# Block 0's transposes, logits and dispatch in blocks 1 to 4, two pairs' scores in block 1, weights converted in place

## The chip, the cores and the metric

One Trainium2 chip, one core. The time is the device time of one execution in microseconds, as the median of several runs. The engines of the core: TensorE (PE; PEld is its weight load), VectorE (DVE), ScalarE (ACT), GpSimd (POOL) and SyncE (SP), which here only issues DMA transfers. Each engine works through its own instructions in program order and waits where an operand or a buffer isn't ready.

## The reference

q, k, v are cut into chunks of 64 tokens; each chunk attends to itself only. The attention output (4608 tokens by 512) runs through a layer `w_in` (512 by 2048) with a sigmoid gate and `w_out` (2048 by 512), and then through a "soft" mixture of experts with 32 slots:

```python
h = x @ w_in
g = h * (1.0 / (1.0 + np.exp(-1.702 * h)))
x = g @ w_out
logits = x @ phi
d = softmax of logits over the tokens (axis 0)       # dispatch weights
slot_input = d.T @ x                                  # 32 slots, 4 for each of 8 experts
slot_out = relu(slot_input[e] @ w1[e]) @ w2[e]        # for each expert e
c = softmax of logits over the slots (axis 1)
out = c @ slot_out
```

The weights `w_in` and `w_out` arrive as 64-bit floats and are turned into 32-bit ones on the chip.

## The kernel before

The 4608 tokens are worked in 12 blocks of 384 (`T`). A block has three attention pairs (128 tokens each) and 16 products f = 0 to 15 (`gemm`, L288), one for each 128 columns of `w_in`. A product is 12 matmuls: x and the weights are split into a high and a low part, and three of the four combinations are summed in one of three PSUM tiles "h" (L292 to L294). ACT takes tanh of it (L296), DVE forms g (L297): the evacuation. In blocks 1 to 10 DVE then transposes g in squares of 32 (L307, `store_g`), and after four products SP writes them to DRAM. `w_out` is never multiplied with g directly: `wp` = w_out times phi gives the logits from g (`logits`, L353), and the dispatch sums g itself with the weights d (`dispatch`, L486, after `load_g`, L322, has read the transposed g back).

What is put between the products is written out by hand, in strings: `HEAD` before block 0, `SIDE0`, `SIDE1` and `SIDE2` for blocks 0 to 2 (key: the product behind which the steps stand), and `PLAN` for blocks 2 to 10. The order of every engine and of SP's queue is that order (`manual_schedule`). The steps, in the strings' letters:

- `P a,c` (`pair_step`, L767): the scores of pair a on PE (L216), the values of pair c (L267), both in one PSUM tile "sx" of which there is a single one; then on DVE maximum and difference for a (L227, L228: "the scores" on DVE), on SP the load of the next q and k, and for c ACT's copy xh (L282) and DVE's xl (L283). "-" leaves a side out.
- `e` (`attn_e`, L233): exp on ACT (L235), three small sums on DVE (L237 to L240), the scaling of e on POOL (L241). `b` (`attn_b`, L245): four transposes on PE (L252) into the PSUM tile "m" (a single one) and ACT's copy pt_sb (L254).
- `Li`, `Lo`: loads of tiles of w_in and w_out (`load_w`, L133) into staging tiles. `i`, `I`, `j` (`w_in_a`, `_b`, `_c`): convert a w_in tile (ACT L119, DVE L123 and L126) and split it (ACT L155, POOL L156); block 0 does this for product f + 3 to f + 5. `o` (`wp_a`, L162): the same conversion of a w_out tile (L119, L123, L126).
- `c`, `d` (`wp_c`, `wp_d`): w_out times phi for four converted tiles (L168), in the PSUM tile "m", ACT's copy (L172), then eight matmuls (L179) again in "m" and a copy to `wp` (L182).
- `t` (`store_g` of block 0), `k` (logits of block 0), `l` (logits of block 1), each for four products; `S0` to `S4` (`slots_0` to `slots_b`): the softmax of one block, of which S0 begins with two matmuls in "m" (L378); `g` and `D`: load_g and dispatch of block 0; `s`: a small selection matrix (L762).

The softmax over tokens is carried from block to block: `stat[b]` holds the maximum and the sum so far, and block b rescales with those of block b - 1. In before, block 0 goes first. `w` in `PLAN` (`more_wo`) loads and converts one more tile of w_out in its second layout; in blocks 2 to 9 that happens four times a block (two loads, two conversions). The w_in staging tiles and the split weights share 17 tiles (`wpool`); w_out staging tiles, x, and the transposed g share 11 (`slab`). Converted weights go to six tiles "cv" (`NCV`).

Of the kernel before, what the change touches and what calls it, by code (L numbers as in the profile page):

```python
# [52 lines left out]
def attention_moe_softmoe_kernel(  # L53
# [84 lines left out]
    def conv(kind, f):
        v = pro[0].tile([128, DM], F32, tag="cv", name="cv", bufs=NCV)
        to_f32(v, stg.pop((kind, f)))  # L140
        return v

    iv = {}
# [768 lines left out]
```

## Time and profile before

| | us |
|---|---|
| median of 3 runs (664.71 to 664.84) | 664.83 |
| span of the profiled execution | 664.1 |
| PE busy | 620.1 (93%) |
| DVE busy | 455.0 (69%) |
| ACT busy | 225.3 (34%) |
| POOL busy | 92.2 (14%) |

The times of the runs are those of whole executions; the span is that of one profiled execution from its first to its last instruction. In the profile PE's matmuls overlap (a matmul of 384 columns shows about 0.33 us, and the next one starts 0.17 us later), so what a step costs on PE is read from the starts, not from the durations. A row of the timeline is: start, duration, engine, line, operation, out<-in, shape and count, and in brackets the idle time before it with what ended it.

### The profile page before, as it was taken

The page shows a single profiled execution, that of the slowest core. Times are in us where ns is not written, and L with a number is a line of the kernel's source. Part 1 is how long each engine was busy: PE and PEld are TensorE (multiplying, and loading weights), DVE is VectorE, ACT ScalarE, POOL GpSimd, SP SyncE. Part 2 cuts the span into 40 slices and gives each one's busy share as a digit, 9 for nine tenths or more (in the row PEclk, how much of TensorE's full clock was granted, in tenths as well). Part 3 has the DMA queues.
Part 4 walks back from the last instruction along what each step waited for, and adds up shares of the span by engine and source line. Part 5 has one row for each costly group of instructions (what it writes and reads, how often), then busy time and mean ns, then how long its engine had stood idle before and what let it go on. Part 6 is the DMA issues. An engine that isn't in the chain of part 4 may idle for free.

```text
span 664.1 us, 15558 instructions
## 1 busy us (share of the span) xinstructions
PE 620.1 (93%) x6414; PEld 523.4 (79%) x6414; DVE 455.0 (69%) x975; ACT 225.3 (34%) x471; POOL 92.2 (14%) x117
## 2 busy tenths in 40 slices
PE   4887999999999999999999999999999999979883
PEld 3776865798889897998998979989989798726552
DVE  5798789797858778677787786777876736331033
ACT  3646544333323233333332333333323322121132
POOL 0355200000101000000010000000101112232410
PEclk9999999999999999999999999999999999998997
DMA  9943867669968567496585774965838879789997
GB/s 345 355 144 112 298 210 224 188 167 333 312 200 330 145 228 269 129 316 196 160 332 141 228 272 129 324 188 161 333 87 267 272 250 389 287 291 375 404 416 310
DMA packets 66055, 167.94 MB, mean 253 GB/s; under 512 B 12544, under 2 KB 36224, under 8 KB 65984
## 3 DMA queue, kind: packets, MB, share of 16 engines
q1 hardware_dynamic: 57376, 129.72, 58.6%
q0 software_dynamic: 8608, 37.23, 14.8%
q8 instruction: 50, 0.82, 0.5%
q14 instruction: 21, 0.17, 0.1%
HBM read 122.29 MB, written 44.63 MB: 251 GB/s over the span
## 4 chain that ended last, share of the span: by engine, by line
PE 81%; DVE 9%; ACT 3%; issue 2%; DMA 2%; SPq 0%; POOL 0%; DVEq 0%; ACTq 0%
PE h L292 19%; PE h L294 18%; PE h L293 18%; PE lp L358 5%; PE dtg L492 5%; PE sx L216 3%; PE h1p L653 3%; DVE cv L126 2%; PE sx L267 2%; PE fp L673 2%; PE pt L252 2%; DVE cv L123 2%; DVE gt L297 1%; PE op L706 1%; DMA v<-in_v_dram 1%
## 5 line engine op out<-in xcount | busy, mean ns | idle before, releaser
L292 PE MATMUL h<-xh,w 128*128 128x384 f32 x768 | 266.5, 347 | 2.7 <-ACT w L155 2.2
L294 PE MATMUL h<-xh,w 128*128 128x384 f32 x768 | 258.9, 337 | 5.5 <-POOL w L156 5.5
L293 PE MATMUL h<-xl,w 128*128 128x384 f32 x768 | 258.2, 336 | 0.0
L296 ACT ACTIVATE gt<-h 128x384 f32<-128x384 f32 x192 | 94.0, 490 | 221.5 <-PE h L294 221.3
L292 PEld LDWEIGHTS h<-xh,w 128*128 128x128 f32 x768 | 144.9, 189 | 23.3 <-issue 17.8
L297 DVE SCALAR_TENSOR_TENSOR gt<-gt,h 128x384 f32<-128x384 f32 x192 | 104.9, 547 | 82.1 <-ACT gt L296 81.8
L294 PEld LDWEIGHTS h<-xh,w 128*128 128x128 f32 x768 | 144.8, 189 | 8.0 <-POOL w L156 7.1
L293 PEld LDWEIGHTS h<-xl,w 128*128 128x128 f32 x768 | 145.0, 189 | 0.2 <-DVE xl L283 0.2
L307 DVE STREAM_TRANSPOSE g<-gt 128x384 f32<-128x384 f32 x176 | 100.2, 574 | 5.4
L241 POOL TENSOR_TENSOR e<-e,rs 128x512 f32<-128x512 f32 x33 | 34.5, 1044 | 415.9 <-DVE rs L240 410.5
L282 ACT ACTIVATE xh<-sx 128x512 fp32r<-128x512 f32 (+1 forms) x38 | 21.6, 575 | 96.0 <-DVE e L228 82.4
L283 DVE TENSOR_TENSOR xl<-sx,xh 128x512 fp32r<-128x512 f32 (+1 forms) x38 | 25.0, 661 | 25.3 <-ACT xh L282 23.8
L565 POOL DMA_DIRECT2D w<-in_moe_w_dram x56 | 29.8, 533 | 87.0 <-PE h L294 36.2
L358 PE MATMUL lp<-gt,wp 128*32 128x384 f32 x384 | 36.8, 492 | 0.1
L492 PE MATMUL dtg<-g,dt 128*32 128x512 f32 x288 | 33.2, 594 | 1.4 <-DVE dt L450 1.4
L126 DVE SCALAR_TENSOR_TENSOR cv<-stg,cv 128x512 uint32<-128x512 uint32 x32 | 29.7, 928 | 1.1
L156 POOL TENSOR_TENSOR w<-cv,w 128x512 fp32r<-128x512 f32 x16 | 24.2, 1525 | 37.9 <-ACT w L155 37.9
L227 DVE TENSOR_REDUCE mx<-sx 128x8 f32<-128x512 f32 (+1 forms) x37 | 23.9, 645 | 5.7 <-PE sx L216 5.7
L228 DVE TENSOR_TENSOR e<-sx,mx 128x512 f32<-128x512 f32 (+1 forms) x37 | 25.1, 677 | 1.8
L252 PE MATMUL pt<-ident,e 128*128 128x128 f32 x144 | 23.1, 285 | 3.4 <-DVE e L241 3.2
L715 DVE COPY o<-op 128x512 f32<-128x512 f32 (+1 forms) x20 | 11.1, 630 | 21.1 <-PE op L706 21.1
L492 PEld LDWEIGHTS dtg<-g,dt 128*32 128x32 f32 x288 | 9.0, 110 | 19.6 <-issue 17.9
(117 smaller groups left out, 554.7 us busy)
## 6 DMA issues: line engine op xcount, KB each, us to landing
g_dram<-g SPq DMA_DIRECT2D x176, 192.0 KB, 3.8
g<-g_dram SPq DMA_DIRECT2D x44, 768.0 KB, 8.9
w<-in_moe_w_dram POOLq DMA_DIRECT2D x34, 512.0 KB, 8.7
qk<-in_qk_dram SPq DMA_DIRECT2D x30, 512.0 KB, 5.5
w<-in_moe_w_dram POOLq DMA_DIRECT2D x17, 768.0 KB, 7.8
stg<-in_moe_w_in_dram SPq DMA_DIRECT2D x16, 512.0 KB, 8.4
stg<-in_moe_w_out_t_dram SPq DMA_DIRECT2D x16, 512.0 KB, 6.1
wo<-in_moe_w_out_dram SPq DMA_DIRECT2D x16, 512.0 KB, 3.7
```

Of the source, the lines that this page charges most:

```text
L126: nc.vector.scalar_tensor_tensor(out=a.bitcast(U32), in0=u[:, :, 0], scalar=29, in1=a.bitcast(U32), op0=ALU.logical_shift_right, op1=ALU.b ...
L241: (nc.gpsimd if pool else nc.vector).tensor_tensor(out=e, in0=e, in1=rs.to_broadcast([128, 2 * KD, 64]), op=ALU.mult)
L252: nc.tensor.transpose(p[:, hp, :], e[:, 2 * hp:2 * hp + 2, :].rearrange("p h k -> p (h k)"), ident)
L292: nc.tensor.matmul(out=h, lhsT=a, rhs=xh[b][:, k, :], start=(k == 0), stop=False)
L293: nc.tensor.matmul(out=h, lhsT=a, rhs=xl[b][:, k, :], start=False, stop=False)
L294: nc.tensor.matmul(out=h, lhsT=l, rhs=xh[b][:, k, :], start=False, stop=(k == KD - 1))
L296: nc.scalar.activation(out=t, in_=h, func=ACTF.Tanh, scale=0.851)
L297: nc.vector.scalar_tensor_tensor(out=t, in0=t, scalar=1.0, in1=h, op0=ALU.add, op1=ALU.mult)
L307: nc.vector.transpose(out=g1[b, q][:, :, :, 32 * j:32 * (j + 1)], in_=t.rearrange("p (a b c) -> p b a c", b=4, c=32))
L358: nc.tensor.matmul(out=lp[b][32 * j:32 * (j + 1), :], lhsT=wp[:, f, :], rhs=gt[b, f], start=(g == 0), stop=(g == NG - 1),)
L492: nc.tensor.matmul(out=p[32 * j:32 * (j + 1)], lhsT=dt[:, i, :], rhs=g[j][i], start=(i == 0), stop=(i == NCP - 1))
L565: eng.dma_start(out=t[:, 0:at], in_=w12[:, w_at[0]:w_at[0] + at])
```

## The change

- Pairs 6 and 7: their scores (`P6`, `P7`) move from products 9 and 12 of block 0 to products 0 and 2 of block 1, their softmax (`e6`, `e7`) and `b6` with them; `P8`'s place stays.
- `w_out` conversions `o0` to `o15` are spread, about one behind every product of block 1 (before: two a product, done by product 8). `c0` to `c2` and `d0` to `d2` follow at products 5 to 14, `c3` and `d3` in block 2.
- Block 0's transposes `t` leave block 1: ten stand in block 2, six in block 3. Its logits `k` stand in block 2 at products 8 and 12, its softmax at the end of block 3 and the start of block 4 (S0 behind b3 of block 3), its dispatch at product 4 of block 4.
- The running softmax now begins with block 1, and block 0 comes between blocks 2 and 3 (`FIRST`, `BEFORE`).
- Weights are converted in place: L119 writes back into every second word of the staging tile, L123 works on these, L126 writes the result to the tile's lower half; the "cv" tiles are gone. Six of the w_out loads go into three new tiles ("p"), the others as before into `slab` ("r").
- The tiles of the first stages live to the end of block 3 (`NPRO`), so the second-layout conversions start in block 4, with six instead of four calls a block (`w4`, `w5`).

```diff
-PLAN = (('b1', 2), ('w2', 2), ('w3', 2), ... ('S1', 7), ('p3', 8), ...
-NCV = 6
+PLAN = (('b1', 2), ('w2', 2), ('w3', 2), ... ('S1', 7), ('w4', 7), ('w5', 7), ('p3', 8), ...
+FIRST = 1
+BEFORE = {2: 1, 0: 2, 3: 0}
+NPRO = 4
 SIDE0 = {
...
-    7: "e5 b4 Li13", 8: "Li14 q7", 9: "P6,4 Li15 v7", 10: "e6 b5", 11: "Lo0r", 12: "P7,5 Lo1r", 13: "e7 b6 Lo2r", 14: "Lo3r",
-    15: "Lo4r",
+    7: "e5 b4 Li13", 8: "Li14 q7", 9: "P-,4 Li15 v7", 10: "b5", 11: "Lo0r", 12: "P-,5 Lo1r", 13: "Lo2r", 14: "Lo3r", 15: "Lo4r",
 }
 SIDE1 = {
-    0: "o0 o1 Lo5r Lo6r", 1: "s o2 o3 Lo7r Lo8r", 2: "b7 c0 o4 o5 Lo9r Lo10r", 3: "d0 o6 o7 Lo11r Lo12r", 4: "P8,6 k0 l0 c1 o8 Lo13r",
-    5: "e8 d1 o9 o10 Lo14r Lo15r", 6: "o11 o12", 7: "c2 o13 o14 t0 t1", 8: "P9,7 k1 l1 d2 o15", 9: "e9 c3 t2 t3 t4", 10: "b8 d3 t5 t6 t7",
-    11: "t8 t9", 12: "P10,8 k2 k3 l2 t10", 13: "e10 b9 t11 t12", 14: "S0 t13 t14", 15: "S1 t15",
+    0: "P6,- o0 Lo5p", 1: "e6 o1 s Lo6p", 2: "P7,- o2 Lo7p", 3: "e7 b6 o3", 4: "P8,6", 5: "e8 b7 c0 o4 Lo8r Lo9r", 6: "d0 o5 l0 Lo10r Lo11r",
+    7: "o6", 8: "P9,7 o7", 9: "e9 b8 c1 o8 Lo12r Lo13p", 10: "d1 o9 l1 Lo14p Lo15p", 11: "o10", 12: "P10,8 o11", 13: "e10 b9 c2 o12",
+    14: "d2 o13 l2", 15: "o14 o15",
 }
-SIDE2 = {0: "S2 g", 1: "S3", 3: "S4", 8: "D"}
+SIDE2 = {
+    0: "c3", 1: "d3 t0", 2: "t1", 3: "t2", 5: "t3", 6: "t4", 7: "t5", 8: "k0 k1", 9: "t6", 10: "t7", 12: "k2 k3", 14: "t8", 15: "t9",
+}
+SIDE3 = {1: "t10", 3: "t11", 5: "t12", 7: "t13", 8: "t14", 10: "t15", 13: "S0 G", 14: "S1", 15: "S2"}
+SIDE4 = {0: "S3", 1: "S4", 4: "D"}
...
-    def to_f32_a(a, st):
-        f = st.bitcast(F32).rearrange("p (n w) -> p n w", w=2)
-        nc.scalar.activation(out=a, in_=f[:, :, 1], func=ACTF.Prelu, scale=2.0 ** -112, alpha=-(2.0 ** 32))
+    def to_f32_a(st):
+        f = st.bitcast(F32).rearrange("p (n w) -> p n w", w=2)[:, :, 1]
+        nc.scalar.activation(out=f, in_=f, func=ACTF.Prelu, scale=2.0 ** -112, alpha=-(2.0 ** 32))
     def to_f32_b(a, st):
         u = st.bitcast(U32).rearrange("p (n w) -> p n w", w=2)
-        nc.vector.tensor_scalar(
-            out=a.bitcast(U32), in0=a.bitcast(U32), scalar1=3, scalar2=None, op0=ALU.logical_shift_left
-        )
+        nc.vector.tensor_scalar(out=u[:, :, 1], in0=u[:, :, 1], scalar1=3, scalar2=None, op0=ALU.logical_shift_left)
         nc.vector.scalar_tensor_tensor(
-            out=a.bitcast(U32), in0=u[:, :, 0], scalar=29, in1=a.bitcast(U32),
+            out=a.bitcast(U32), in0=u[:, :, 0], scalar=29, in1=u[:, :, 1],
             op0=ALU.logical_shift_right, op1=ALU.bitwise_or,
         )
+    def low(st):
+        return st.bitcast(F32)[:, 0:DM]
...
     def wp_a(q):
-        ov[q] = conv("o", q)
+        st = stg.pop(("o", q))
+        to_f32(low(st), st)
+        ov[q] = low(st)
...
             elif kind == "w":
-                if 1 < b < 10:
+                if NPRO <= b < 10:
                     more_wo()
...
-            if b < 3:
-                start((SIDE0, SIDE1, SIDE2)[b].get(f, ""))
+            if b < 5:
+                start((SIDE0, SIDE1, SIDE2, SIDE3, SIDE4)[b].get(f, ""))
```

## Rows read from the trace of the kernel before

**Rows 1.** The page: span, and PE's busy tenths in 40 equal slices.
```profile
span 664.1 us, 15558 instructions
...
PE   4887999999999999999999999999999999979883
```

**Rows 2.** PE's timeline: third matmul of product 9 in block 0; block 1; block 2.
```profile
53.57 0.44 PE L294 MATMUL h<-xh,w 128*128 128x384 f32 x1 [1.24 <-POOL w L156]
...
75.69 0.33 PE L292 MATMUL h<-xh,w 128*128 128x384 f32 x1
...
77.77 0.33 PE L292 MATMUL h<-xh,w 128*128 128x384 f32 x1
...
136.14 0.33 PE L292 MATMUL h<-xh,w 128*128 128x384 f32 x1
```

**Rows 3.** PE's timeline in block 1: b7, c0, d0, P8,6, logits, c1.
```profile
81.94 0.60 PE L252 MATMUL pt<-ident,e 128*128 128x128 f32 x4
83.22 1.05 PE L168 MATMUL wpp<-cv,acc 128*32 128x512 f32 x4 [0.69 <-ACT pt_sb L254]
...
88.72 0.97 PE L179 MATMUL wps<-sel,psb 128*128 128x32 f32 x8
89.53 0.42 PE L292 MATMUL h<-xh,w 128*128 128x384 f32 x1
...
91.79 0.69 PE L216 MATMUL sx<-qk 64*64 64x64 f32 x32
92.31 0.65 PE L267 MATMUL sx<-pt_sb,v 64*64 64x64 f32 x32
92.89 1.50 PE L358 MATMUL lp<-gt,wp 128*32 128x384 f32 x16
94.20 1.04 PE L168 MATMUL wpp<-cv,acc 128*32 128x512 f32 x8
```

**Rows 4.** DVE's timeline in block 1.
```profile
78.49 0.56 DVE L297 SCALAR_TENSOR_TENSOR gt<-gt,h 128x384 f32<-128x384 f32 x1 [1.52 <-ACT gt L296]
...
79.59 0.39 DVE L123 TENSOR_SCALAR cv<-cv 128x512 uint32<-128x512 uint32 x1
80.01 0.69 DVE L126 SCALAR_TENSOR_TENSOR cv<-stg,cv 128x512 uint32<-128x512 uint32 x1
80.62 0.42 DVE L123 TENSOR_SCALAR cv<-cv 128x512 uint32<-128x512 uint32 x1
...
94.21 0.65 DVE L227 TENSOR_REDUCE mx<-sx 128x8 f32<-128x512 f32 x1
94.90 0.69 DVE L228 TENSOR_TENSOR e<-sx,mx 128x512 f32<-128x512 f32 x1
96.34 0.69 DVE L283 TENSOR_TENSOR xl<-sx,xh 128x512 fp32r<-128x512 f32 x1 [0.75 <-ACT xh L282]
...
99.52 0.64 DVE L237 TENSOR_REDUCE sm<-e 128x8 f32<-128x512 f32 x1
...
102.29 0.41 DVE L123 TENSOR_SCALAR cv<-cv 128x512 uint32<-128x512 uint32 x1
```

**Rows 5.** POOL's timeline in block 0.
```profile
65.69 3.19 POOL L156 TENSOR_TENSOR w<-cv,w 128x512 fp32r<-128x512 f32 x2
```

**Rows 6.** DVE's timeline in block 0, the same stretch.
```profile
67.75 1.67 DVE L126 SCALAR_TENSOR_TENSOR cv<-stg,cv 128x512 uint32<-128x512 uint32 x1
```

**Rows 7.** PE's timeline in block 3: b3 and what follows.
```profile
223.27 0.60 PE L252 MATMUL pt<-ident,e 128*128 128x128 f32 x4
223.63 0.42 PE L292 MATMUL h<-xh,w 128*128 128x384 f32 x1
```

**Rows 8.** ACT's timeline in block 3, the same stretch.
```profile
223.86 0.63 ACT L235 ACTIVATE e<-e 128x512 f32<-128x512 f32 x1
224.38 0.59 ACT L254 ACTIVATE pt_sb<-pt 128x512 f32<-128x512 f32 x1
```

**Rows 9.** Busy us of each engine in a steady stretch; PE, PEld, DVE, ACT, POOL.
```profile
220.00:264.00 44.00, 44.00 (x454) 39.33 (x450) 33.50 (x74) 15.20 (x32) 3.13 (x3) 1.00 0.67 221
```

More of the change, by code (lines that the diff above doesn't have):

```diff
@@ L113, in to_f32, with load_w @@
     def to_f32(a, st):
-        to_f32_a(a, st)
+        to_f32_a(st)
         to_f32_b(a, st)
-    def to_f32_a(a, st):
-        f = st.bitcast(F32).rearrange("p (n w) -> p n w", w=2)
-        nc.scalar.activation(out=a, in_=f[:, :, 1], func=ACTF.Prelu, scale=2.0 ** -112, alpha=-(2.0 ** 32))
+    def to_f32_a(st):
+        f = st.bitcast(F32).rearrange("p (n w) -> p n w", w=2)[:, :, 1]
+        nc.scalar.activation(out=f, in_=f, func=ACTF.Prelu, scale=2.0 ** -112, alpha=-(2.0 ** 32))
     def to_f32_b(a, st):
         u = st.bitcast(U32).rearrange("p (n w) -> p n w", w=2)
-        nc.vector.tensor_scalar(
-            out=a.bitcast(U32), in0=a.bitcast(U32), scalar1=3, scalar2=None, op0=ALU.logical_shift_left
-        )
+        nc.vector.tensor_scalar(out=u[:, :, 1], in0=u[:, :, 1], scalar1=3, scalar2=None, op0=ALU.logical_shift_left)
         nc.vector.scalar_tensor_tensor(
-            out=a.bitcast(U32), in0=u[:, :, 0], scalar=29, in1=a.bitcast(U32),
+            out=a.bitcast(U32), in0=u[:, :, 0], scalar=29, in1=u[:, :, 1],
             op0=ALU.logical_shift_right, op1=ALU.bitwise_or,
         )
+    def low(st):
+        return st.bitcast(F32)[:, 0:DM]
     pro, stg, w_t = {}, {}, {}
-    def load_w(kind, f, in_slab):
-        t = (slab_tile if in_slab else w_tile)([128, DM], I64, "stg")
+    def load_w(kind, f, place):
+        if place == "r":
+            t = slab_tile([128, DM], I64, "stg")
+        elif place == "p":
+            t = pro[0].tile([128, DM], I64, tag="o", name="stg", bufs=3)
+        else:
+            t = w_tile([128, DM], I64, "stg")
         nc.sync.dma_start(out=t, in_=(w_in if kind == "i" else w_out_t)[:, f, :])
         stg[kind, f] = t
[L138 to L143, printed above, removed]
     def w_in_a(f):
-        iv[f] = pro[0].tile([128, DM], F32, tag="cv", name="cv", bufs=NCV)
-        to_f32_a(iv[f], stg["i", f])
+        to_f32_a(stg["i", f])
     def w_in_b(f):
-        to_f32_b(iv[f], stg.pop(("i", f)))
+        to_f32_b(low(stg["i", f]), stg["i", f])
     def w_in_c(f):
-        v = iv.pop(f).rearrange("p (k c) -> p k c", k=KD)
+        v = low(stg.pop(("i", f))).rearrange("p (k c) -> p k c", k=KD)
         t = w_tile([128, 2, KD, 128], F32R, "w")
@@ L354, in logits @@
         if g == 0:
-            lp[b] = ps.tile([128, T], F32, tag="lp" if b % 2 else "pt", name="lp")
+            lp[b] = ps.tile([128, T], F32, tag="lp" if b % 2 or b == 0 else "pt", name="lp")
         for j in range(4):
@@ L367, in logits @@
                 return
-            lps[b] = [mid_tile([128, T], f"lps{i}", F32R) for i in range(2)]
+            lps[b] = [
+                mid_tile([128, T], f"lps{i}", F32R) if b else pro[0].tile([128, T], F32R, tag="gt", name="lps0", bufs=NF)
+                for i in range(2)
+            ]
             nc.scalar.activation(out=lps[b][0], in_=p, func=ACTF.Copy)
@@ L395, in slots_1 @@
         cr = None
-        if b > 0:
+        if b != FIRST:
             cr = st_p.tile([128, 1], F32, tag="cr", name="cr")
-            nc.scalar.activation(out=cr, in_=stat[b - 1][0], func=ACTF.Exp, scale=-1.0, bias=nm)
+            nc.scalar.activation(out=cr, in_=stat[BEFORE.get(b, b - 1)][0], func=ACTF.Exp, scale=-1.0, bias=nm)
         sm_t[b] = d, nm, s, cr
@@ L494, in dispatch @@
                 )
-        if b == 0:
+        if b == FIRST:
             nc.vector.tensor_copy(acc, p)
@@ L579, in more_wo @@
     def more_wo():
-        fn, i = wo_list.pop(0)
-        fn(i)
+        if wo_list:
+            fn, i = wo_list.pop(0)
+            fn(i)
     def at(key):
@@ L798, in start @@
         once = {
-            "phi": start_wp, "z": start_const, "s": start_sel, "g": lambda: load_g(0), "D": lambda: dispatch(0),
+            "phi": start_wp, "z": start_const, "s": start_sel, "G": lambda: load_g(0), "D": lambda: dispatch(0),
         }
         for x in steps.split():
-            k, n = x[0], x[1:].rstrip("r")
+            k, n = x[0], x[1:].rstrip("rp")
             if x in once:
@@ L805, in start @@
             elif k == "L":
-                load_w(x[1], int(n[1:]), x[-1] == "r")
+                load_w(x[1], int(n[1:]), x[-1])
             elif k in "AC":
@@ L838, in attention_moe_softmoe_kernel @@
             start(HEAD)
-            block(0)
-            block(1)
+            for b in range(NPRO):
+                block(b)
     with tc.tile_pool(name="spare", bufs=NSPARE) as pro[1]:
@@ L843, in attention_moe_softmoe_kernel @@
             more_wo()
-            for b in range(2, NB - 1):
+            for b in range(NPRO, NB - 1):
                 block(b)
```

10 lines of the change are left out of this document (5 added, 5 removed).

## The prediction

> **What bounds the kernel now.** I read the page first, then TensorE's timeline block by block, then the three engines that feed it. The span is 664.1 us [rows 1]; the median of the runs shown is 664.83, so 0.73 us lie around the span, and I carry that over unchanged. In the slices of [rows 1] TensorE is full from the ninth slice to the thirty-fifth; only the head, the early blocks and the tail have gaps. Since the change touches neither head, steady blocks nor tail in their order, what it can win lies in blocks 0 and 1.
>
> A product of a block (12 matmuls of `gemm`) takes 77.77 - 75.69 = 2.08 us [rows 2]. Block 1 runs from 75.69 to 136.14, which is 60.45 us. Its work, from start-to-start distances in [rows 3]: pair (scores and values) 92.89 - 91.79 = 1.10, scores alone 0.52, values alone 0.58; one `b` (four transposes) 223.63 - 223.27 = 0.36 [rows 7]; one `c` 1.04; one `d` 0.81; a logits group (94.20 - 92.89) / 2 = 0.66. Two plain matmuls of S0 are 2 x 2.08 / 12 = 0.35. So 16 x 2.08 + 3 x 1.10 + 3 x 0.36 + 4 x 1.04 + 4 x 0.81 + 7 x 0.66 + 0.35 = 50.0, and **10.4 us are waits** (restarts after an insertion, some 0.1 each, are left in; they stay in the sum after too). They sit at the `c` steps: c0 waits for pt_sb, the copy that empties b7's PSUM tile, and then for DVE's conversions [rows 3].
>
> In block 0 I take the stretch from the third matmul of product 9 (53.57) to block 1, 22.12 us [rows 2]. Ten matmuls of product 9 (1.73), 6 x 2.08, 2 x 1.10 and 2 x 0.36 are 17.1, so **5.0 us are waits**, for weights that are still being split (POOL's L156, as in the 1.24 us that end at 53.57).
>
> TensorE's work as a whole does not change: every matmul that leaves a block comes back in another. So the time changes by waits after minus waits before; 15.4 us of waits before are open to it.
>
> **Prices on DVE** [rows 4]. Evacuation and transposition of one product 79.59 - 78.49 = 1.10, the first starting 78.49 - 77.77 = 0.72 after the product's end (ACT's tanh lies between). Conversion of one w_out tile 80.62 - 79.59 = 1.03. Scores (L227, L228) 1.38. Then ACT copies xh, and L283 ends 96.34 + 0.69 - 95.59 = 1.44 after L228. Softmax sums with a conversion behind them 102.29 - 99.52 = 2.77: while POOL scales e, the two-input L126 is held up. The same holding is seen in block 0: while POOL's two L156 take 3.19 us [rows 5], an L126 takes 1.67 instead of 0.69 [rows 4, 6].
>
> **Part 1: block 0 loses the scores of pairs 6 and 7 and two softmaxes.** That is 2 x (1.38 + 1.01) = 4.8 us of DVE work, and 2 of POOL's multiplications. More than the sum, it is an order that goes: in product 9 ACT copies xh only after DVE's new scores in the same PSUM tile (the 0.75 idle before L283 [rows 4] shows the copy queued between the two), and the splitting of weights is queued behind that copy. With values alone the copy needs no scores. The wait up to 53.57 comes from pair 5, which stays, and is counted on neither side. For products 9 to 11 DVE does an evacuation (half of 1.10), a conversion (1.03) and is held by one L156 (half of 3.19 less the part beside the evacuation, some 1.2): 2.8 a product against 2.1 to 2.7 on TensorE. Over three products that leaves 0.5 to 2; with the last split ending behind the last conversion I take 1.8 instead of 5.0 us: **-3.2**.
>
> **Part 2: block 1.** DVE loses block 0's transposes, all 16, some 8 us (half of 1.10 each), and gains 4.8 us of scores and softmax. The sum falls, but the order decides. I walk from the block's start (TensorE and DVE from 0). First evacuation at 2.8. Product 0: 1.10 + 1.38 + 1.03 = 3.5. Product 1: 1.10 + 2.77 and 0.5 for sel = 4.4. Product 2: 3.5. Product 3: 1.10 + 2.77 = 3.9. DVE is then at 18.1, and reads P8's scores at 18.1 + 1.10 + 1.38 = 20.6. TensorE needs for products 0 to 4 with P6, P7, b6 and P8 only 5 x 2.08 + 2 x 0.52 + 0.36 + 1.10 = 12.9. Behind the scores ACT has, in its order, copy xh, tanh of product 5, exp of e8, and the copy of b7's tile: four steps at the 0.52 distance of [rows 8], so 22.7. c0 may start only then: it uses the single PSUM tile "m" that b7 has filled (the pt_sb wait of [rows 3] is this one, with no exp before it). TensorE's own work up to c0 is 12.9 + 2.08 + 0.36 = 15.3: 7.4 us lost with restarts. c0 ends at 23.7. Products 6, 7, 8 with d0 and l0 follow, 7.9 with restarts, to 31.6. c1 has the same neighbours (P9, e9, b8): 0.72 + 1.10 + 1.38, then five ACT steps (copy xh, o7's first step, tanh, exp, copy) at the same distance make 5.8, so c1 starts at 37.4, where TensorE was free at 35.2. One turn later c2 starts at 38.4 + 7.9 + 5.8 = 52.1, ends at 53.2, and products 14, 15 with d2 and l2 (5.7) close the block at 58.9. Its work is 16 x 2.08 + 2 x 0.52 + 3 x 1.10 + 4 x 0.36 + 3 x 1.04 + 3 x 0.81 + 3 x 0.66 = 46.6. Waits **12.3 instead of 10.4: +1.9**.
>
> **Part 3: blocks 2 to 4.** c3 (block 2, product 0) needs o14 and o15, both put behind product 15: 0.72 + 1.10 + 2 x 1.03 = 3.9 after its end, where TensorE is ready after 2.08: **+1.9**. S0 of block 0 now stands right behind b3 in block 3, again on tile "m": b3's transposes end at 223.63, the copy ends at 224.38 + 0.59 = 224.97 [rows 7, 8], with exp before it: **+1.4**. The ten, then six transposes (0.5 each), the logits groups and the dispatch are work without a wait: block 2 and 3 have no weight conversions of w_out any more (2 x 1.03 fewer each), and DVE is idle for a quarter of a steady block (33.50 of 44 us busy [rows 9]). Three conversions in blocks 4 to 8 instead of two are covered by the same idle time (if it were gone, 1 us a block at most). The loads of block 0's g are queued on SP behind block 3's last stores of block 0, four products ahead of use; if they were late, the dispatch would wait, and only it.
>
> **Part 4: in place.** L123 reads and writes every second word. The trace has no such row. Nearest is L123 itself, 0.39 (same count, packed); the other end is L126, which reads with that step and takes 0.69. Below nothing I see no reason. I take L123's own row, cost 0. A staging tile is held one step longer; w12 to w15 then go into tiles that POOL has read one product before, 2 us ahead: cost 0, up to 1 us if POOL is late. Loads Lo8 and Lo9 wait on SP for c0's tiles, to 23.7; they are needed past 37, which leaves 13 us for a transfer.
>
> [...]
>
> **Sum.** Waits after 1.8 + 12.3 + 1.9 + 1.4 = 17.4, before 15.4: **+2.0 us**, span 666.1, median 666.8 (0.3% slower).
>
> **Rivals.** (a) L123 falls to 0.69: 0.3 x 16 = 4.8 us on a DVE that sets c0 to c3 in block 1; block 0 hardly changes, since L123 there waits for POOL anyway. 4 to 5 us of it show: some 671.5. For it: nothing in the trace excludes it. (b) Faster: DVE keeps pace at P8. The 7.4 us before c0 come from DVE's 17.8 us for products 0 to 4 against TensorE's 12.9. If conversions and softmax sums overlapped so that P8's scores were read at 15 instead of 20.6, c0 would wait 5.5 us less, and the time would be 661.3; it is a gain as soon as more than 2.0 us go there. Against it: the prices are start-to-start distances, with nothing left between; for it: block 1 has 3 us less DVE work in all. (c) No change: parts 1 and 2 cancel; each of the terms may be off by 1 us, which gives 663.5 to 666.1. (d) The change does not do what it says, because w_out tiles land late and conversions wait for DMA: up to 5 us more, 672; the slack of 13 us above speaks against it.
>
> **How the numbers follow.** Forecast (666.2 to 669) 0.41; (a) 0.18; (b) 0.20; (c) 0.18; (d) 0.03. Slower by over 0.2% (1.3 us, about what a measurement of this kernel can tell): 0.41 + 0.18 + 0.03 = 0.62. Within: 0.18. Faster: 0.20. The range goes from (b)'s 661.3 to 672, leaving a tenth at each end; the likeliest case alone is 665.5 to 669.
>
> **What would show it.** Right: block 1 starts near 71, lasts near 59, with c0 starting some 5 us after b7's transposes behind pt_sb; c1 and c2 wait 2 us each; S0's matmul starts 1.4 us after b3's in block 3. Wrong: L123 at 0.69 in the changed kernel (a); c0 right behind b7 and block 1 under 55 us (b); ACT waiting for w_out loads (d). A wait of TensorE beyond block 4 would be a thing I did not see.

## The result and the profile after

The changed kernel takes 675.15 us (median of four runs, 672.85 to 677.89) against 664.79 (664.71 to 664.84) before: a ratio of 1.0149 with a 95% interval of 1.0133 to 1.0166. It is slower, as forecast, but by 10.4 us where 2.0 were forecast.

The lines of the code have moved by a few: L119 is now L124, L123 L128, L126 L129, L168 L173, L179 L184, L252 L257, L254 L259, L292 to L294 L297 to L299, L358 L363, L378 L386.

The page of the changed kernel: span, PE's busy tenths and the clock granted to PE, in 40 slices. It answers to [rows 1].

```profile
span 673.5 us, 15546 instructions
...
PE   3888968899999999999999999999999999988883
...
PEclk9999978899999999999999999999999999999997
```

The head, the steady blocks and the tail look as they did. Slices six to eight (84 to 135 us) have a hole, and in the same slices the granted clock is down to seven and eight tenths; all three lie in block 1. From the starts of PE's first matmul of each block:

| | before | forecast | after |
|---|---|---|---|
| block 1 starts | 75.69 | 71.1 | 71.24 |
| block 1 lasts | 60.45 | 58.9 | 67.45 |
| block 2 lasts | 47.29 | 51.05 | 51.28 |
| block 3 lasts | 44.45 | 46.15 | 46.23 |
| block 4 lasts | 44.32 | 47.0 | 46.88 |
| block 5 starts | 272.20 | 274.2 | 283.08 |

(The forecasts of blocks 2 to 4 are the lengths before with the steps of the prediction's part 3 put in: c3, d3, ten and six transposes, logits, S0 and dispatch.) One block is wrong, by 8.5 us, and all the others are within 0.25.

PE's timeline of the changed kernel in block 1, from its first matmul to that of block 2. It answers to [rows 3].

```profile
71.24 0.33 PE L297 MATMUL h<-xh,w 128*128 128x384 f32 x1
...
88.76 0.66 PE L257 MATMUL pt<-ident,e 128*128 128x128 f32 x4 [0.21 <-POOL e L246]
93.76 2.12 PE L173 MATMUL wpp<-stg,acc 128*32 128x512 f32 x8 [4.35 <-ACT pt_sb L259]
95.82 0.69 PE L297 MATMUL h<-xh,w 128*128 128x384 f32 x1
96.31 0.52 PE L298 MATMUL h<-xl,w 128*128 128x384 f32 x1
96.62 0.52 PE L299 MATMUL h<-xh,w 128*128 128x384 f32 x1
...
99.39 0.33 PE L299 MATMUL h<-xh,w 128*128 128x384 f32 x1
99.56 0.97 PE L184 MATMUL wps<-sel,psb 128*128 128x32 f32 x8
100.90 0.85 PE L363 MATMUL lp<-gt,wp 128*32 128x384 f32 x8 [0.37 <-ACT wp L187]
101.69 0.44 PE L297 MATMUL h<-xh,w 128*128 128x384 f32 x1
...
111.92 1.65 PE L173 MATMUL wpp<-stg,acc 128*32 128x512 f32 x8 [1.98 <-ACT pt_sb L259]
...
129.29 1.95 PE L173 MATMUL wpp<-stg,acc 128*32 128x512 f32 x8 [1.96 <-ACT pt_sb L259]
...
138.69 0.33 PE L297 MATMUL h<-xh,w 128*128 128x384 f32 x1
```

The waits are those of the forecast: c0 starts 93.76 - 71.24 = 22.5 us into the block (forecast 22.7), 5.0 us behind b7's transposes and behind pt_sb; c1 and c2 wait 1.98 and 1.96 us (forecast 2). What is new stands *behind* each wait. Of a product, one matmul starts 96.62 - 96.31 = 0.31 us after the other, where 0.17 is the rule; c0 itself takes 95.82 - 93.76 = 2.06 us instead of the 1.04 of [rows 3]. The distance is back at 0.17 from 99.39 on.

The same kernel in stretches of 10 us: busy time of PE, PEld, DVE, ACT and POOL, then PE's granted clock, DMA's share and GB/s.

```profile
80.00:90.00 10.00, 8.28 (x104) 7.20 (x103) 9.69 (x18) 2.56 (x5) 1.93 (x2) 1.00 0.58 171
90.00:100.00 10.00, 6.24 (x25) 4.58 (x25) 5.39 (x11) 3.38 (x7) 1.04 (x1) 0.66 0.61 194
100.00:110.00 10.00, 9.57 (x117) 8.25 (x116) 6.73 (x13) 3.34 (x8) 0.00 (x0) 1.00 0.62 190
110.00:120.00 10.00, 7.71 (x41) 5.87 (x42) 7.09 (x14) 4.39 (x9) 1.04 (x1) 0.83 0.79 251
120.00:130.00 10.00, 8.04 (x108) 7.22 (x107) 7.09 (x14) 4.08 (x8) 0.00 (x0) 1.00 0.66 189
130.00:140.00 10.00, 9.63 (x54) 7.72 (x49) 5.04 (x12) 3.64 (x8) 1.04 (x1) 0.83 0.03 12
```

The stretches with c0 and c1, and the one behind the start of c2 (129.29), have a mean clock under 1.00; the stretches between are at 1.00. Before, no stretch of block 1 was under 1.00; two of its stretches, of the kernel before:

```profile
80.00:90.00 10.00, 9.10 (x48) 6.17 (x47) 8.47 (x18) 5.13 (x11) 0.00 (x0) 1.00 0.67 222
...
100.00:110.00 10.00, 8.94 (x103) 5.80 (x106) 9.48 (x20) 4.31 (x8) 1.04 (x1) 1.00 0.68 229
```

In shorter stretches the granted clock is 0.50 from 92.5 to 99.0 us and 1.00 again from 99.25 on; behind the start of c1 it is 0.50 from 113.0 to 116.25, behind that of c2 from 130.0 to 133.25, and 1.00 ahead of these stretches and behind them. The rows agree, with 0.31 to 0.33 us between matmuls of 384 columns at 0.50 and 0.17 at 1.00, so 0.66 is a mean over time at these two values.

A second, smaller new row is the logits' wait, 0.37 us for the copy behind `d` (L187). It comes with each of l0 to l2, since `l` stands right behind its `d`.

Why c0 is late, on DVE and ACT of the changed kernel:

```profile
90.94 0.69 DVE L233 TENSOR_TENSOR e<-sx,mx 128x512 f32<-128x512 f32 x1
```

```profile
91.72 0.60 ACT L287 ACTIVATE xh<-sx 128x512 fp32r<-128x512 f32 x1 [5.28 <-DVE e L233]
92.22 0.49 ACT L301 ACTIVATE gt<-h 128x384 f32<-128x384 f32 x1
92.59 0.63 ACT L240 ACTIVATE e<-e 128x512 f32<-128x512 f32 x1
93.11 0.60 ACT L259 ACTIVATE pt_sb<-pt 128x512 f32<-128x512 f32 x1
```

DVE ends P8's scores at 91.63, 20.4 us into the block (forecast 20.6), and ACT does its four steps behind them: copy, tanh, exp, and the copy that gives the PSUM tile "m" back to c0. The walk of the prediction is in these rows step for step. Its price for what TensorE does afterwards is not.

### The profile page after: what moved, and what is told of

Read it like the earlier page. It is cut to its first block, busy times and chain, and to the rows that moved or that the text cites. A ratio compares the mean times of both kernels' runs of the same rounds, so it can differ in the third digit from the quotient of the medians.

```text
span 673.5 us, 15546 instructions
## 1 busy us (share of the span) xinstructions
PE 623.5 (93%) x6414; PEld 526.4 (78%) x6414; DVE 457.8 (68%) x975; ACT 226.1 (34%) x471; POOL 91.3 (14%) x117
## 3 DMA queue, kind: packets, MB, share of 16 engines
q1 hardware_dynamic: 57376, 129.72, 58.1%
## 4 chain that ended last, share of the span: by engine, by line
PE 81%; DVE 10%; ACT 4%; issue 2%; DMA 1%; POOL 0%; SPq 0%; DVEq 0%; ACTq 0%
PE h L297 19%; PE h L299 18%; PE h L298 18%; PE lp L363 5%; PE dtg L500 5%; DVE stg L129 3%; PE sx L221 2%; PE sx L272 2%; PE fp L682 2%; PE h1p L662 2%; PE pt L257 2%; DVE stg L128 2%; DVE gt L302 2%; PE wpp L173 1%; PE op L715 1%
## 5 line engine op out<-in xcount | busy, mean ns | idle before, releaser
L297 PE MATMUL h<-xh,w 128*128 128x384 f32 x768 | 268.2, 349 | 1.5 <-ACT w L158 1.0
L299 PE MATMUL h<-xh,w 128*128 128x384 f32 x768 | 260.1, 339 | 3.9 <-POOL w L159 3.8
L297 PEld LDWEIGHTS h<-xh,w 128*128 128x128 f32 x768 | 146.1, 190 | 24.7 <-issue 20.3
L302 DVE SCALAR_TENSOR_TENSOR gt<-gt,h 128x384 f32<-128x384 f32 x192 | 105.0, 547 | 86.9 <-ACT gt L301 86.4
L299 PEld LDWEIGHTS h<-xh,w 128*128 128x128 f32 x768 | 145.9, 190 | 6.6 <-POOL w L159 5.8
L363 PE MATMUL lp<-gt,wp 128*32 128x384 f32 x384 | 37.0, 492 | 1.2 <-ACT wp L187 1.1
L129 DVE SCALAR_TENSOR_TENSOR stg<-stg 128x512 uint32<-128x512 uint32 x32 | 30.9, 966 | 1.1
L159 POOL TENSOR_TENSOR w<-stg,w 128x512 fp32r<-128x512 f32 x16 | 23.1, 1449 | 36.0 <-ACT w L158 36.0
L257 PE MATMUL pt<-ident,e 128*128 128x128 f32 x144 | 23.2, 286 | 3.9 <-DVE e L246 3.2
```

The lines of the kernel that those rows point to most:

```text
L129: nc.vector.scalar_tensor_tensor(out=a.bitcast(U32), in0=u[:, :, 0], scalar=29, in1=u[:, :, 1], op0=ALU.logical_shift_right, op1=ALU.bitwi ...
L257: nc.tensor.transpose(p[:, hp, :], e[:, 2 * hp:2 * hp + 2, :].rearrange("p h k -> p (h k)"), ident)
L297: nc.tensor.matmul(out=h, lhsT=a, rhs=xh[b][:, k, :], start=(k == 0), stop=False)
L299: nc.tensor.matmul(out=h, lhsT=l, rhs=xh[b][:, k, :], start=False, stop=(k == KD - 1))
L302: nc.vector.scalar_tensor_tensor(out=t, in0=t, scalar=1.0, in1=h, op0=ALU.add, op1=ALU.mult)
L363: nc.tensor.matmul(out=lp[b][32 * j:32 * (j + 1), :], lhsT=wp[:, f, :], rhs=gt[b, f], start=(g == 0), stop=(g == NG - 1),)
```

## The experiments

All times are medians; "before" ran beside each on the same chip, with 664.9 to 665.7 us. A *slot* is the distance from the first matmul of a product to that of the next, with all that stands between. The ladder first, then the clock, then what the waits hang on.

**One part of the change at a time: in place alone.** The kernel before, with the conversion functions of the kernel after and nothing else.

```diff
-        ov[q] = conv("o", q)
+        st = stg.pop(("o", q))
+        to_f32(low(st), st)
+        ov[q] = low(st)
...
-    def to_f32_a(a, st):
+    def to_f32_a(st):
```

> The kernel before with the conversion in place alone, everything else as before (staging tiles are held until the split or the c step). Theory: L123 and L126 keep their durations on every second word (0.39 to 0.43 and 0.69); 664.8, within 0.7. Rival: staging tiles that come free later delay the w_out loads, conversions wait for DMA, 1 to 4 us slower.

Measured: 666.73 us (ten runs), 1.0018 [1.0004, 1.0032] of before: 1.0 us more, at the edge of what can be told. It does not lie in the shift. All instructions of that line on staging tiles in the kernel after, and of its counterpart before; duration min/median/max in ns:

```profile
L128 DVE TENSOR_SCALAR stg<-stg x32: 377/422/1399, 14.4 to 141.5; 128x512 uint32<-128x512 uint32 x32
```

```profile
L123 DVE TENSOR_SCALAR cv<-cv x32: 374/420/1061, 14.4 to 114.8; 128x512 uint32<-128x512 uint32 x32
```

Rival (a) falls: on every second word the operation takes 422 ns in the median, packed it took 420. (On the 16 tiles of the second layout the medians are 388 in place alone and 389 before.)

Where the 1.0 us lies can be read in one execution of each. Block 1 starts 0.80 us earlier in place than before (74.89 against 75.69) and lasts 1.84 us longer (62.29 against 60.45). In it a transposition on DVE stands 1.61 us until PE is done with c1; ACT's copy psb comes later for that, and d1 waits 0.87 us for the copy. Before, neither of the two waits. In place alone (L168 of before is L163 there, L307 is L302):

```profile
94.49 0.58 DVE L302 STREAM_TRANSPOSE g<-gt 128x384 f32<-128x384 f32 x1 [1.61 <-PE wpp L163]
```

```profile
97.61 1.08 PE L174 MATMUL wps<-sel,psb 128*128 128x32 f32 x8 [0.87 <-ACT psb L167]
```

In place, the converted weights lie in the staging tile itself, so a `slab` tile comes free only behind the `c` that reads it, and this transposition is given one of those. Before, the tile was free behind its conversion. So tiles do come free later, as the rival of the expectation had it, but it is DVE that waits and not a load. The next run, which has the same order, shows the same two waits (0.97 and 0.86 us). The clock does not show as the reason: product 9 of block 0 takes 6.31 us in place and 4.91 before, at a granted clock of 0.82 and 1.00 between 50 and 55 us, but block 1 starts no later for it, and over all runs the mean granted clock is 0.990 in both kernels.

**The transposes, logits, softmax and dispatch of block 0 alone** (with in place, and with the tiles of the first stages living to the end of block 3): the order of blocks 0 and 1 as before, without block 0's `t`, `k`, S0 and S1 in block 1.

```diff
+    0: "o0 o1 Lo5r Lo6r", 1: "s o2 o3 Lo7r Lo8r", 2: "b7 c0 o4 o5 Lo9r Lo10r", 3: "d0 o6 o7 Lo11r Lo12r", 4: "P8,6 l0 c1 o8 Lo13r",
+    5: "e8 d1 o9 o10 Lo14r Lo15r", 6: "o11 o12", 7: "c2 o13 o14", 8: "P9,7 l1 d2 o15", 9: "e9 c3", 10: "b8 d3",
+    12: "P10,8 l2", 13: "e10 b9",
```

> The changed kernel with block 0 and block 1 in the order of the kernel before (pairs 6 and 7 in block 0, w_out conversions two a product, c0 to c3 at products 2, 4, 7, 9), so that only block 0's transposes, logits, softmax and dispatch are moved and the conversion is in place. Theory: the waits at c0 (3.2 us) and c2 (3.1) stand ahead of the transposes and stay; block 1 loses its 3 us of moved work and a wait of 1 to 2 us: 55.5; S0 costs 1.5 in block 3; 664 to 666, no change. Rival (DVE's transposes were what held block 1): block 1 under 52, 660 to 661.

Measured: 667.83 us, 1.0037 [1.0024, 1.0051], above the 664 to 666 expected. Taking 16 transposes off DVE shortens block 1 from 60.45 to 59.03 us only. Four logits groups (2.6 us of PE by the prediction's 0.66) and S0 left with them, so against before the waits there did not get shorter at all; against in place alone (62.29) block 1 is 3.26 us shorter, of which 3.0 are the work that left. Blocks 2 to 4 take the work up, and S0 its wait behind b3.

**The pairs back in block 0**: the kernel after, with P6, P7, their softmax and b6 where they stood before.

```diff
-    ... 9: "P-,4 Li15 v7", 10: "b5", 11: "Lo0r", 12: "P-,5 Lo1r", 13: "Lo2r", ...
+    ... 9: "P6,4 Li15 v7", 10: "e6 b5", 11: "Lo0r", 12: "P7,5 Lo1r", 13: "e7 b6 Lo2r", ...
-    0: "P6,- o0 Lo5p", 1: "e6 o1 s Lo6p", 2: "P7,- o2 Lo7p", 3: "e7 b6 o3", ...
+    0: "o0 Lo5p", 1: "o1 s Lo6p", 2: "o2 Lo7p", 3: "o3", ...
```

> The changed kernel with the scores and softmax of pairs 6 and 7 back in block 0 as before. By the walk through DVE's queue: DVE reaches P8's scores some 6 us earlier, c0's wait falls from 4.4 to about 2.3 us, the waits at c1 and c2 stay at 2; block 1 shorter by 4 to 5 us with its work (1.1 us of scores, 0.36 of b6), block 0 longer by 4.5 to 5. So 674 to 676, no gain. Rival (the two pairs are what makes the change slow): 666 to 670.

Measured: 670.67 us, 1.0072 [1.0052, 1.0091]. That is 4.5 us less than with the pairs moved, so the expectation of the theory is missed and the rival nearly right. Block 0 gets 3.6 us longer (block 1 starts at 74.80), and block 1 8.4 us shorter (59.05). Of these 8.4, the two slots of c0 and d0 alone are 15.51 - 10.38 = 5.1. c0 waits 2.06 us there instead of 4.35, and this time the clock stays up behind it (behind c1 and c2, which wait 1.95 and 1.96 us in the same execution, it does not: 0.90, 0.93 and 0.83 in the stretches of 10 us from 100 to 130):

```profile
91.24 1.25 PE L173 MATMUL wpp<-stg,acc 128*32 128x512 f32 x8 [2.06 <-ACT pt_sb L259]
```

```profile
90.00:100.00 10.00, 8.40 (x54) 6.83 (x55) 6.21 (x13) 4.55 (x10) 1.05 (x1) 1.00 0.82 289
```

The ladder, each step against the one above: in place +1.0, transposes and dispatch moved +1.1, conversions and `c` spread one behind every product +2.8 (670.67 - 667.83), pairs moved +4.5. Their sum is the 9 to 10 us of the change, and every rung is a loss. The last rung is not the pairs' work alone: part of it is the clock, which fell behind c0 in the one kernel and not in the other.

**The clock by itself.** The kernel after, with 24, 12 and 12 matmuls of 384 columns that nobody reads, in the waits before c0, c1 and c2; they go into PSUM tile "pt", which lies unused there.

```diff
-    ... 5: "e8 b7 c0 o4 Lo8r Lo9r", ... 9: "e9 b8 c1 o8 Lo12r Lo13p", ... 13: "e10 b9 c2 o12",
+    ... 5: "e8 b7 f24 c0 o4 Lo8r Lo9r", ... 9: "e9 b8 f12 c1 o8 Lo12r Lo13p", ... 13: "e10 b9 f12 c2 o12",
+    def fill(n):
+        p = ps.tile([128, T], F32, tag="pt", name="fill")
+        for i in range(n):
+            nc.tensor.matmul(out=p, lhsT=w_t[0][:, 0, 0, :], rhs=xh[1][:, 0, :], start=True, stop=True)
```

> The changed kernel with matmuls that nobody reads put into the three long waits of block 1 (24 of 384 columns before c0, 12 before c1 and 12 before c2, into the PSUM tile that is free there). They fill 4.2 and twice 2.1 us of waits of 4.4, 2.0 and 2.0 us, so c0, c1 and c2 can start when they did. [...] Theory B (the waits alone make the loss, the clock is not affected by what stands in them): same as the changed kernel, 675, block 1 67 to 68.

Measured: 671.09 us, 1.0076 [1.0054, 1.0098]: 4.1 us less than the kernel after (4.9 by the ratios to before), by adding work. Block 1 falls from 67.45 to 61.97; I had expected about 61, and a time of about 669, if the lower clock was the loss. Its timeline at c0 and its stretches:

```profile
89.07 4.41 PE L804 MATMUL fill<-xh,w 128*128 128x384 f32 x24
93.66 1.25 PE L173 MATMUL wpp<-stg,acc 128*32 128x512 f32 x8 [0.18 <-ACT pt_sb L259]
94.85 0.45 PE L297 MATMUL h<-xh,w 128*128 128x384 f32 x1
95.13 0.34 PE L298 MATMUL h<-xl,w 128*128 128x384 f32 x1
95.31 0.35 PE L299 MATMUL h<-xh,w 128*128 128x384 f32 x1
```

```profile
90.00:100.00 10.00, 9.45 (x62) 7.56 (x61) 7.44 (x15) 4.50 (x9) 1.05 (x1) 1.00 0.70 219
...
110.00:120.00 10.00, 9.63 (x96) 7.92 (x92) 6.93 (x14) 3.98 (x8) 1.04 (x1) 1.00 0.62 223
...
130.00:140.00 10.00, 9.86 (x51) 6.58 (x52) 5.97 (x12) 3.34 (x7) 0.00 (x0) 1.00 0.33 80
```

c0 starts at the same moment (93.66, and 93.76 without the filling), so the wait is not shorter; but the clock is 1.00 in every stretch, c0 takes 1.19 us instead of 2.06, and the product behind it has its 0.17 again. The six slots at c0 to d2 fall by 0.86, 1.53, 0.27, 1.28, 0.56 and 1.00, together 5.5 us. This is the cost of the lower clock in block 1.

**The logits' wait by itself.** The filled kernel, with l0 to l2 one product later.

```diff
-    6: "d0 o5 l0 ...", 7: "o6", ... 10: "d1 o9 l1 ...", 11: "o10", ... 14: "d2 o13 l2", 15: "o14 o15",
+    6: "d0 o5 ...", 7: "l0 o6", ... 10: "d1 o9 ...", 11: "l1 o10", ... 14: "d2 o13", 15: "l2 o14 o15",
```

> The kernel with unread matmuls in the waits before c0 to c2, with l0 to l2 each one product later than d0 to d2. Theory: the logits' wait for the copy behind d (0.37 us of idle time, three times) costs with its restart about 0.5 us each, so each slot with d loses 0.5 beyond the logits' own 0.66, block 1 goes from 62.0 to about 60.4 and the time from 671.1 to about 669.5. Rival: only the idle 0.37 is lost, three times: block 1 60.9, time 670.0; or the wait moves to the next matmul and nothing is gained: 671.

Measured: 668.58 us, 1.0053 [1.0038, 1.0068], 2.5 us less than filled alone (1.5 by the ratios to before). Block 1 is 60.74 instead of 61.97, expected 60.4; each pair of slots d and l falls by 0.49 (4.34 + 2.19 to 3.00 + 3.04). Three small waits of 0.37 are worth 0.4 to 0.5 us each.

**The waits taken away: c, d and l one product later.**

```diff
-    ... 5: "e8 b7 c0 o4 Lo8r Lo9r", 6: "d0 o5 l0 Lo10r Lo11r", 7: "o6", 8: "P9,7 o7", 9: "e9 b8 c1 o8 Lo12r Lo13p", ...
+    ... 5: "e8 b7 o4", 6: "c0 o5 Lo8r Lo9r", 7: "d0 o6 l0 Lo10r Lo11r", 8: "P9,7 o7", 9: "e9 b8 o8", 10: "c1 o9 ...", ...
```

> The changed kernel with c0 to c3, d0 to d3 and l0 to l2 one product later (c and b no longer behind the same product). [...] Rival: DVE's queue sets the length of block 1 whatever the order of TensorE's steps is; block 1 stays above 58, waits move to the evacuation of the products, 666 to 670.

Measured: 663.39 us, 0.9956 [0.994, 0.9972]: faster than before. Block 1 is 56.83. I had expected 661 to 664 us with no wait over 1 us left in block 1. The time is in that range, but a wait is left: c0, behind a whole product more, still waits 2.25 us for pt_sb and starts at 93.88, where it started in the kernel after. DVE's lateness at P8 is that large. c1 and c2 wait no more.

**The same, with b7 to b9 in the other PSUM tile.**

```diff
-            p = ps.tile([128, KD, 128], F32, tag="m" if cp >= NCP else "pt", name="pt")
+            p = ps.tile([128, KD, 128], F32, tag="m" if cp >= NCP and cp not in (7, 8, 9) else "pt", name="pt")
```

> The kernel with c, d and l one product later, and besides b7 to b9 in the other PSUM tile, so that c0 has no tile to wait for. Theory: c0's wait behind pt_sb (2.3 us) and the clock at its lower level behind it go together: c0's two slots fall from 5.94 and 5.60 us to about 4.2 and 4.3, or, if c0 then waits a little for VectorE's conversion, the first is 4.2 to 5.2; block 1 falls from 56.8 to 54 to 55 us. In block 2 no transposition has to wait for a buffer that the products of the same block still read (as it does with c and d in the other tile), so block 2 stays at 50.5. Time 663.4 less 2.5: about 661. Rival: the conversion of o3 or o7 on VectorE is as late as the tile was, c0 waits 2 us for it instead, and the time stays at 663.

Measured: 661.6 us, 0.9942 [0.9928, 0.9957]. Block 1 is 53.84. c0 has no wait left; d0 now waits 0.36 us for ACT's copy psb. First without, then with the other tile:

```profile
90.00:100.00 10.00, 7.42 (x38) 5.87 (x36) 8.69 (x16) 4.90 (x11) 1.06 (x1) 0.83 0.64 204
```

```profile
90.00:100.00 10.00, 9.27 (x84) 6.87 (x87) 8.94 (x18) 5.49 (x12) 1.06 (x1) 1.00 0.61 198
```

A wait of 2.25 us in this place went, and 3.0 us of block 1 with it: again more than the wait, and again with the clock.

**c and d in the other PSUM tile, in the kernel after.**

```diff
-        part = ps.tile([128, 512], F32, tag="m", name="wpp")
+        part = ps.tile([128, 512], F32, tag="pt", name="wpp")
-        p = ps.tile([128, 4, NS], F32, tag="m", name="wps")
+        p = ps.tile([128, 4, NS], F32, tag="pt", name="wps")
```

> The changed kernel with the c and d steps in a PSUM tile of their own (the one that is free in block 1), order unchanged. If the tile shared with b makes c0 wait, c0 starts right behind b7 and o3 (wait 0.2 instead of 4.4), but d0 then waits 1.5 to 2 us for c0's copy, which ACT has queued behind xh, tanh and exp; c1 and c2 wait for o7 and o11, as long as before: 670 to 672. Rival (c0 waits for o3, not for the tile): same as the changed kernel, 675.

Measured: 675.22 us, 1.0137 [1.0119, 1.0156], where 670 to 672 was expected. Block 1 did fall, to 61.36 us: c0 starts 0.6 us behind b7, d0 then waits 1.54 us for ACT's copy psb. But block 2 grew from 51.28 to 58.11. DVE and PE of this kernel at its end:

```profile
172.55 0.52 DVE L302 SCALAR_TENSOR_TENSOR gt<-gt,h 128x384 f32<-128x384 f32 x1
181.34 0.58 DVE L312 STREAM_TRANSPOSE g<-gt 128x384 f32<-128x384 f32 x1 [8.27 <-PE h L298]
```

```profile
180.96 0.33 PE L298 MATMUL h<-xl,w 128*128 128x384 f32 x1
```

My first reading was a tile still held by one of eight stores that SP had queued just before. To test it, t7 with its four stores was put two products later:

```diff
-    ... 9: "t6", 10: "t7", 12: "k2 k3", ...
+    ... 9: "t6", 12: "k2 k3 t7", ...
```

> The kernel with c and d in the other PSUM tile, with one step more: t7 of block 0 (and with it the four stores of its group) stands behind product 12 of block 2 instead of product 10, so that these stores do not stand in one row with the four stores of block 2's own group on SP. Theory: the 8.3 us that VectorE stood before a transposition at 181.34 there were a wait for a tile that such a store still held; then product 15's slot of block 2 falls from 11.7 back to about 4.9 us, block 2 from 58.1 to about 51.3, and the time is 668 to 669.5. Rival: the wait has nothing to do with the neighbouring stores (another transfer held the tile); then block 2 stays near 58 and the time near 675.

Measured: 675.18 us, 1.0145 [1.0126, 1.0163]; the wait stays (8.73 us, block 2 57.93), so the stores are not it. It ends 48.5 us after the block's start in both kernels, at the end of the block's last matmul on xl (180.96 + 0.33), which is the line that the row names as its releaser. In the kernel after, the evacuation at the same place, 178.39 - 138.69 = 39.7 us into the block, has its transposition right behind it, at 178.94.

By that releaser, the `slab` tile handed to this transposition is one that the running block's own products still read (xl lies in `slab`); the trace does not name the tile. DVE stands until they are done, ACT's copy and the next softmax stand behind DVE, and the dispatch waits 4.25 us at product 15. Block 2 grows by 6.83 us, more than that wait, and again the clock is down behind it:

```profile
180.00:192.00 12.00, 7.75 (x39) 3.17 (x38) 8.34 (x17) 3.13 (x7) 1.04 (x1) 0.72 0.31 94
```

By this reading, changing a PSUM tag has changed which of the 11 tiles is handed out; why is not in the trace. A version of this experiment without that side effect was not tried in the kernel after; with c, d and l later (above) there is no such wait, and block 2 is 50.49.

**Three versions that go on from "c, d and l later".** In the first, the pairs are also back in block 0 and S0 of block 0 uses tile "pt"; in the second the pairs stay moved, c0 stands at product 7, d0 and l0 at 8, and S0 uses "pt"; the third adds b7 to b9 in "pt" to this.

```diff
-        lg = ps.tile([128, T], F32, tag="m", name="lg")
+        lg = ps.tile([128, T], F32, tag="m" if b else "pt", name="lg")
-    ... 6: "c0 o5 Lo8r Lo9r", 7: "d0 o6 l0 Lo10r Lo11r", 8: "P9,7 o7", ...
+    ... 6: "o5", 7: "c0 o6 Lo8r Lo9r Lo10r Lo11r", 8: "d0 l0 P9,7 o7", ...
```

> The run "later" with pairs 6 and 7 back in block 0 as before, and S0 of block 0 in the free PSUM tile. Block 0 lasts 3.5 us longer (its start of block 1 at 74.8 as in "pairsback"), block 1 has 1.5 us less work and DVE no backlog, so c0 in product 6 waits for nothing: 48 us instead of 56.8. Theory A: 656 to 658, no better than moving c0 alone, so the move of the two pairs is worth nothing by itself. Rival (the two pairs' move is the gain of the change): 661 or more.

> The run "later" with c0 and d0 one product later again (products 7 and 8; l0 with d0) and S0 of block 0 in the PSUM tile that is free in block 3. Theory A: the last long wait of block 1 (2.3 us at c0, with product and c0 behind it at half clock, 4.8 us in all) goes, and S0's 1.5; block 1 52 us instead of 56.8, the time 657 (656 to 658.5), 1% under the kernel before. Rival (DVE's queue sets the length of block 1): c0's wait moves to the evacuations, block 1 stays over 55, 661 to 662.

> The kernel with c0 at product 7, d0 and l0 at 8, the other c, d and l one product later and S0 of block 0 in the other PSUM tile, and besides b7 to b9 in the other PSUM tile. Theory: what is left of waits for the tile (0.2 and 1.2 us before c0 and c1) goes, block 1 falls from 54.3 to about 53.0, time 658.6. Rival: c1 then waits for VectorE's conversion just as long: 659.9.

Of the diff, the first two lines are in all three, the last two make the second version.

Measured: 660.1 us (0.9921 [0.9908, 0.9933]), 659.92 us (0.9923 [0.9911, 0.9935]) and 659.75 us (0.9922 [0.9905, 0.9938]). All three beat both kernels, by 0.8% against before, and cannot be told apart. With most waits out of the way, moving the pairs shows no gain (the first two versions also differ in c0's place by one product): block 0 is 3.8 us shorter with it (71.14 against 74.90), block 1 5.1 us longer (54.26 against 49.19), of which 1.4 is the work that moved, and the times are the same. The 656 to 658.5 expected of the first two were not reached; block 1 was to take 48 and 52 us and takes 49.19 and 54.26. In the third, c1 waits 0.5 us for DVE's conversion in place of 1.2 for the tile, and d1 and l1 give it back: the rival's time was right, though its wait was half as long. S0's own tile is worth 1.2 of the 1.4 us that its wait was priced at: its slot in block 3 falls from 4.40 to 3.24 us, and in the second version S0 starts right behind b3:

```profile
215.96 0.63 PE L257 MATMUL pt<-ident,e 128*128 128x128 f32 x4
216.34 0.60 PE L386 MATMUL lg<-lps,sel 128*128 128x384 f32 x2
```

## Why the prediction was wrong, and where it was right

**Part 1 held.** Block 1 was to start at 75.69 - 3.2 - 1.4 (the work that leaves) = 71.1 and starts at 71.24. The waits went where it said: behind 53.57 TensorE still waited 3.2 us for weights before (0.86, 1.24, 0.32 and 0.76), and 0.26 us in the kernel after. Undone, it costs 3.6 us of block 0.

**Part 2 failed, in its price for TensorE behind a wait.** The walk of DVE and ACT to c0 was right to 0.2 us, and so were the waits of c1 and c2. The step that failed is "c0 ends at 23.7. Products 6, 7, 8 with d0 and l0 follow, 7.9 with restarts", and its two repetitions. They price TensorE at full clock right behind a wait. From block 1's start:

| | forecast | measured | measured less forecast, of the segment |
|---|---|---|---|
| c0 starts | 22.7 | 22.5 | -0.2 |
| c1 starts | 37.4 | 40.7 | +3.5 |
| c2 starts | 52.1 | 58.1 | +2.7 |
| block ends | 58.9 | 67.5 | +2.6 |

The error comes three times, once behind each wait, and most of it is one term. By the filled kernel 5.5 of the 8.5 us are the lower clock; by that with the logits later, another 1.2 are the logits' wait for the copy behind `d`, which the walk left out (in before, `l` stood apart from its `d`). The remaining 1.8 were not pursued; insertions with more of a restart than the 0.1 that I had kept are a candidate (the slot of a product with one logits group is 3.04 there, against 2.08 + 0.66). I had read before's waits in block 1 and found the clock at 1.00 all through it, and took that for every wait. None of those was as long: the trace names 0.69 us before c0 [rows 3] and at most 1.1 us before the others. (At c0 3.2 us are lost before too: 6.66 of its slot less 2.08, 0.36 and 1.04. But they come in pieces, with some of c0's matmuls between.)

```profile
PE wpp L168 <- DVE cv L126: 1.7, 3, 1.1
PE wps L179 <- ACT pt_sb L254: 0.7, 1, 0.7
PE wpp L168 <- ACT pt_sb L254: 0.7, 1, 0.7
```

The three rows are TensorE's waits in block 1 of the kernel before (us in total, times, the longest); in the kernel after one row is enough, and it is twelve times the last:

```profile
PE wpp L173 <- ACT pt_sb L259: 8.3, 3, 4.3
```

**Part 3 held.** Blocks 2 to 4 are within 0.25 us. c3 stands in a slot of 5.02, against 2.08 + 1.04 of work: 1.9 of wait and restart. S0 starts 231.56 - 230.04 = 1.5 us behind b3, forecast 1.4 [rows 7, 8]; the row of the kernel after:

```profile
230.04 0.63 PE L257 MATMUL pt<-ident,e 128*128 128x128 f32 x4
231.56 0.61 PE L386 MATMUL lg<-lps,sel 128*128 128x384 f32 x2 [0.90 <-ACT pt_sb L259]
```

**Part 4 held for the instruction** (0.42 us); that the step would cost nothing was my estimate from the packed row's 0.39. As a whole it costs 1.0 us in the order of before: it did not see that a tile held until its `c` can be the one that a transposition on DVE is given next. In the kernel after no transposition of block 1 waits for a `c`. Rival (a) is refuted by the rows of L128. Rival (b) is too: DVE read P8's scores at 20.4 us, not at 15. Rival (c) does not hold: even with the clock held up, the filled kernel is 0.8% slower. Rival (d) is refuted, as no `c` in block 1 waits for a transfer.

**The sum.** Block 5 starts at 283.08 instead of the 274.2 that the sum stood for, so 8.9 us are missing there. The last block and the tail took 1.5 us less than before (125.9 against 127.4 from block 11's start); that is in part luck, since before's execution had the lower clock for a moment there (0.90 and 0.93 between 590 and 610 us) and the other had not (1.00 between 600 and 620). And the time around the span was 1.7 us (675.22 of the profiled execution less 673.5), where I had carried 0.73 over from a median. The three make the 8.3 us between 666.8 and 675.15.

The range ended at 672 because each case in it was a wait of some length at full clock; that a wait could cost more than itself was in none of them.

## What to carry to other kernels

A wait of TensorE of some microseconds may not be over when it is over: look at the granted clock in short stretches behind each wait, and price the work behind it at both levels (1.00 and 0.50 here, the lower one for 3 to 7 us). When a step that needs an engine's late result can stand one product later at no cost, put it there; here that alone turned a loss of 10 us into a gain of 2, while filling the wait with idle matmuls gave back 4. Before moving work off an engine, find which single buffer the next stage waits for: block 1's waits hung on one PSUM tile and on the order of ACT's copies, and neither 16 fewer transposes nor two pairs less changed that (with the pairs back, c0 to c2 still waited 2 us each). When a conversion is done in place, ask who else is given that tile, since it comes free only behind its last reader.
